# A rational activation's denominator rewritten as a square plus an absolute value, with two changed loading steps ahead of it, in an attention and two-MLP kernel

## The chip, the cores and the metric

The kernel runs on one core of one Trainium2 chip. The metric is the device time of one execution in microseconds (us). The five queues that matter are TensorE (PE), VectorE (DVE), ScalarE (ACT), GpSimd (POOL) and the DMA queue of SyncE (SP).

## What is computed

Local attention with block summaries feeds a first MLP with a rational activation, and that feeds a second MLP with `h*cos(h)`. The part that the change touches is the rational activation and the two block summaries (a maximum over 32 keys, a mean over 32 values).

```python
k_sum = k.reshape(B, H, nb, block, D).max(axis=3)      # B=2 H=8 S=768 D=64 block=32
v_sum = v.reshape(B, H, nb, block, D).mean(axis=3)
...
h = x @ w_in                                           # 1536 x 512 @ 512 x 2048
h2 = h * h
h3 = h2 * h
P = a[0] + a[1] * h + a[2] * h2 + a[3] * h3
Q = 1.0 + np.abs(b[0]) * np.abs(h) + np.abs(b[1]) * h2
g = P / (Q + 1e-06)
return (g @ w_out).astype(np.float32)
```

## The kernel before

**Stages.** Batch 0's keys are loaded and transposed by `k_pair` (L456), batch 1's by `k_tile`; the value means come from `v_mean0` (L512) and `v_mean1` (L540). Twelve attention units of 128 rows each follow (`attn_a`, `attn_b`, `attn_c`): scores, softmax, transposed probabilities, and the product with the values, whose result is split into a high and a low part (xH, xL) as input of the MLP. The MLP works on units: one of 16 column blocks of 128 of the hidden layer, for one of three tiles of 512 tokens, in each of two layers. The first tile's first four blocks are done in halves of 256 tokens, so that layer 0 has 8 half units and 44 full ones, and layer 1 has 48. `mlp_h` (L789) makes 12 matmuls for a unit, `ew1` (L832) or `ew2` the activation, `split_g` the high and low part of the result, and `mlp_o` (L898) 12 more matmuls. The weights arrive as 64-bit floats and are turned to 32-bit ones by three DVE operations (L765, L769, L773) in `conv`, then split into two parts (L360 and L779, mostly on POOL). Attention units are filled in between the MLP units of the first four blocks.

**The activation before.** `ew1` computes `|b1|*|h|` with ACT's Abs out of PSUM (L839), adds `|b0|` and multiplies by `h` on DVE (L847), takes ACT's Abs of that (L855), and then the logarithm (L857) and the exponential of its negative (L860), which is a first value of 1/Q. DVE refines it (L862, L865). The numerator is a chain beside it: L841 (ACT, or DVE as L843), L850, L852, and L868 multiplies both.

**What sets the order.** Nothing is issued in the order in which the code is written. Every step is registered with `P.op`: the engines that may do it with their costs, what it reads, what it writes. A step that lists a tile among its writes comes after every earlier user of that tile. `Plan.order` is a list scheduler: it works out the latest start of each step, then picks steps by when their engine and buffers are free, and among several engines takes the one with the least finish plus a weight per engine that depends on the time (`WEIGHT`). A cost wrapped in `Shared` (certain DVE steps and all POOL steps) also waits until the last such step is over. `setup` is emitted ahead of the plan. TensorE, ACT, DVE, POOL and SP each execute their own list in order.

Of the kernel before, what the change touches and what calls it, by code (L numbers as in the profile page):

```python
# [29 lines left out]
LAT = {}  # L30
# [54 lines left out]
class Op:  # L85
# [2 lines left out]

    def at(self, e):

        return max((t + LAT[x, e] for t, x in self.after), default=0.0)


class Plan:
# [194 lines left out]
def kernel(  # L289
# [21 lines left out]
    WK = 96  # L311
# [52 lines left out]


    nc.scalar.preload_act_table_set("natural_log_exp_and_others")
    co_r = fixed([128, 8], F32, "co")
    co = co_r.t
    ident_r = fixed([128, 128], F32, "ident")
    ident = ident_r.t  # L370
    a0, a1, a2, a3 = (co[:, i:i + 1] for i in range(4))
    b0a, b1a = co[:, 6:7], co[:, 7:8]

    masks = {off: fixed([128, KW], F32, f"mask{off[0]}{off[1]}") for off in ((0, 16), (16, 16), (16, 32))}
    vsel_r = fixed([128, 40], F32, "vsel")
# [7 lines left out]
    def setup():  # L383
        make_identity(nc, ident)

        wu = pools["pa"].tile([128, 512], F32, tag="acc0", name="warm", bufs=1)
        for i in range(8):
            nc.tensor.matmul(out=wu[:, 0:128], lhsT=ident, rhs=ident, start=True, stop=True)
        nc.sync.dma_start(out=co[:, 0:4], in_=moe_a.partition_broadcast(128))
        nc.sync.dma_start(out=co[:, 4:6], in_=moe_b.partition_broadcast(128))  # L390
        nc.scalar.activation(out=co[:, 6:8], in_=co[:, 4:6], func=ACTF.Abs)
        nc.gpsimd.memset(vsel, 0.0)

        nc.gpsimd.memset(vsel[:, 16:24], 1.0 / 32.0)
        nc.gpsimd.affine_select(out=vsel[:, 16:24], in_=vsel[:, 16:24], pattern=[[-16, 8]],
                                compare_op=ALU.is_ge, fill=0.0, base=0, channel_multiplier=1)
        nc.gpsimd.affine_select(out=vsel[:, 16:24], in_=vsel[:, 16:24], pattern=[[16, 8]],
                                compare_op=ALU.is_ge, fill=0.0, base=15, channel_multiplier=-1)
        for offs in masks:
            m = masks[offs].t  # L400
            nc.gpsimd.memset(m, 0.0)
            nc.gpsimd.memset(m[:, WK:KW], LN32_8)
            for half in range(2):
                off = offs[half]
                mh = m[64 * half:64 * half + 64, 0:WK]

# [49 lines left out]
    def k_pair(pr, lead):  # L456

        if pr == 0:
            kT[0] = new("big", [128, 4096], F32, "big", 2)
        kr = kT[0]  # L460
        kk, ks = k_parts(0)
        room = early_room(pr // 2)
        raw = room["k", pr]
        rt = lambda: room.t[:, 768 * (pr % 2):768 * (pr % 2) + 768].rearrange(
            "p (i h x) -> p i h x", i=3, h=2)
        for h in range(2):
            P.op([("S", 0.7)], [], [raw[h]],
                 lambda e, h=h: nc.sync.dma_start(
                     out=rt()[:, :, h], in_=k[0, 2 * pr + h].rearrange("(i s j) d -> s i (j d)", s=128, j=2)),
                 prio=P.now - lead)  # L470
        for i0, n in ((0, 2), (2, 1)):
            tp = psum([128, 256 * n], "ktp", True)

            def tr(e, tp=tp, i0=i0, n=n):
                for i in range(n):
                    transpose_pairs(tp.t[:, 256 * i:256 * i + 256], rt()[:, i0 + i], 0, 128)

            P.op([("T", 0.44 * n)], [raw[0], raw[1]], [tp], tr)
            P.op([("A", act(256 * n, True)), ("V", dve(256 * n))], [],
                 [tp] + [kr["k", i, pr] for i in range(2 * i0, 2 * i0 + 2 * n)],  # L480
                 lambda e, tp=tp, i0=i0, n=n: cp(e, kk()[:, pr, 256 * i0:256 * (i0 + n)], tp.t))
            P.op([("V", dve(256 * n))], [], [tp, kr["s", pr]],
                 lambda e, tp=tp, i0=i0, n=n: nc.vector.tensor_reduce(
                     out=ks()[:, pr, 8 * i0:8 * (i0 + n)],
                     in_=tp.t.rearrange("p (m t) -> p m t", t=32), axis=AX.X, op=ALU.max))
# [26 lines left out]
    def v_mean0(lead):  # L512

        vp = psum([128, NH * D], "vmp", True)
        room = new("big", [128, 4096], F32, "big", 2)
        for i in range(3):
            raw = room[i]
            P.op([("S", 1.75)], [], [raw],
                 lambda e, i=i: nc.sync.dma_start(
                     out=room.t[:, 1024 * i:1024 * i + 1024].rearrange("p (h x) -> p h x", h=NH),  # L520
                     in_=v[0, :, 256 * i:256 * i + 256, :].rearrange("h (s j) d -> s h (j d)", j=2)),
                 prio=P.now - lead)

            def sel(e, i=i):
                x = room.t[:, 1024 * i:1024 * i + 1024].rearrange("p (h j d) -> p h j d", h=NH, j=2)
                for j in range(2):
                    nc.tensor.matmul(out=vp.t[WK:KW].rearrange("p (h d) -> p h d", h=NH),
                                     lhsT=vsel[:, 16 - 8 * i:40 - 8 * i], rhs=x[:, :, j],
                                     start=i == 0 and j == 0, stop=i == 2 and j == 1)

            P.op([("T", 1.78)], [raw], [vp], sel)
        for i in range(2):
            P.op([("A", act(512, True)), ("V", dve(512))], [], [vp, vws[i]["m"]],
                 lambda e, i=i: cp(e, vws[i].t[WK:KW], vp.t[WK:KW]))
        for vw in vws[2:]:
            P.op([("S", 0.2)], [vws[0]["m"]], [vw["m"]],
                 lambda e, vw=vw: nc.sync.dma_start(out=vw.t[WK:KW], in_=vws[0].t[WK:KW]))
        P.now += 5.3

    def v_mean1(lead):  # L540

# [64 lines left out]
    def attn_a(u):  # L606
# [6 lines left out]
               for y in range(NP)}  # L613
        kw = kws[u % NKW]
        if t < NKW:
            P.op([("P", Shared(0.6)), ("A", act(192))], [kr["s", y] for y in range(NP)], [kw["s"]],
                 lambda e: cp(e, kw.t[:, :, :, WK:KW],
                              ks().unsqueeze(2).to_broadcast([128, NP, 2, NB])))

# [26 lines left out]
        for hh in range(2):  # L646
            sc = new("at", [128, NP, KW], F32, "sc", 4)
            sp = sps[hh]
            for pr in range(NP):
# [6 lines left out]
                         out=sc.t[:, pr, :], in_=sc.t[:, pr, :], func=ACTF.Exp, scale=-1.0,  # L656
                         bias=mn.t[:, hh, pr:pr + 1], accum_out=su.t[:, hh, pr:pr + 1]))
            sus = [su[hh, pr] for pr in range(NP)]
            P.op([("A", 0.11)], [], sus,
                 lambda e, hh=hh: nc.scalar.activation(out=su.t[:, hh], in_=su.t[:, hh],  # L660
                                                       func=ACTF.Identity, bias=1e-9))
            P.op([("V", Shared(0.09))], [], sus,
                 lambda e, hh=hh: nc.vector.reciprocal(out=su.t[:, hh], in_=su.t[:, hh]))
            ss = [sc[pr] for pr in range(NP)]
# [167 lines left out]
    def ew1(un):  # L832
# [3 lines left out]
        H, EE, U, Z = (lambda r=r: r.t[:, 0:n] for r in (h, te, tu, tf))  # L836

        P.op([("A", act(n, True, 1))], [], [h, tu],
             lambda e: nc.scalar.activation(out=U(), in_=H(), func=ACTF.Abs, scale=b1a))  # L839
        P.op([("A", act(n, True, 2)), ("V", dve(n, 2))], [], [h, te],  # L840
             lambda e: (nc.scalar.activation(out=EE(), in_=H(), func=ACTF.Identity, scale=a3, bias=a2)  # L841
                        if e == "A" else
                        nc.vector.tensor_scalar(out=EE(), in0=H(), scalar1=a3, scalar2=a2,  # L843
                                                op0=ALU.mult, op1=ALU.add)))

        P.op([("V", dve(n, 1))], [], [h, tu],
             lambda e: nc.vector.scalar_tensor_tensor(out=U(), in0=U(), scalar=b0a, in1=H(),  # L847
                                                      op0=ALU.add, op1=ALU.mult))
        P.op([("V", dve(n))], [], [h, te],
             lambda e: nc.vector.tensor_tensor(out=EE(), in0=EE(), in1=H(), op=ALU.mult))  # L850
        P.op([("V", dve(n, 1))], [], [h, te],
             lambda e: nc.vector.scalar_tensor_tensor(out=EE(), in0=EE(), scalar=a1, in1=H(),  # L852
                                                      op0=ALU.add, op1=ALU.mult))
        P.op([("A", act(n))], [], [tu],
             lambda e: nc.scalar.activation(out=U(), in_=U(), func=ACTF.Abs))  # L855
        P.op([("A", act(n))], [tu], [tf],
             lambda e: nc.scalar.activation(out=Z(), in_=U(), func=ACTF.Ln, bias=QC))  # L857

# [252 lines left out]
```

## Time and profile before

| | us |
|---|---|
| median of 3 runs | 627.66 |
| lowest, highest | 627.12, 629.93 |
| the profiled execution's own time | 628.18 |
| span of its instructions | 626.5 |

| engine | busy us | share of the span |
|---|---|---|
| PE | 602.1 | 96% |
| PE weight load | 493.3 | 79% |
| DVE | 489.0 | 78% |
| ACT | 394.1 | 63% |
| POOL | 352.3 | 56% |

The span runs from the first to the last instruction on the core; some 1.7 us lie around it. Matmuls are pipelined and their ends are modelled, so PE's busy time counts some time in which PE was not at its peak. The mean granted clock of TensorE was 0.986 of full speed.

### The profile page before, as it was taken

To read this page: it belongs to the slowest core of one execution; us is meant where nothing else is said; L and a number is where in the kernel's file an instruction comes from. 1 tells how busy PE (TensorE), PEld (TensorE's weight loads), DVE (VectorE), ACT (ScalarE), POOL (GpSimd) and SP (SyncE) were. 2 spreads that over 40 slices of the span, in tenths; PEclk is the share of its full clock that TensorE was granted. 3 is DMA by queue.
4 is the path that set the end of the run, shared out by engine and by line. 5 is a ranking of instruction groups with operands and counts; after the bars stand their busy time and mean duration, and the time that the engine had idled before them with its cause. 6 is when DMAs were issued, how large, how long until landed. Compare 5 with 4: busy or idle time off the path is not lost.

```text
span 626.5 us, 9893 instructions
## 1 busy us (share of the span) xinstructions
PE 602.1 (96%) x3522; PEld 493.3 (79%) x3522; DVE 489.0 (78%) x942; ACT 394.1 (63%) x851; POOL 352.3 (56%) x368
## 2 busy tenths in 40 slices
PE   8769897999999999999999999999999999999997
PEld 7458876788788888888888878888888888888886
DVE  2599977677999999999999999758756884773541
ACT  4698878967657665766666765454465446543553
POOL 4356684352556676657736668667536764474332
PEclk9889997999999999999999999999999999999999
DMA  8996975210022131213211323313302230000112
GB/s 215 241 225 167 197 192 138 43 22 1 33 69 67 35 104 65 67 35 101 67 35 37 99 67 101 115 54 101 101 0 69 74 129 1 34 1 0 68 49 86
DMA packets 69737, 51.79 MB, mean 83 GB/s; under 512 B 37288, under 2 KB 63912, under 8 KB 69688
## 3 DMA queue, kind: packets, MB, share of 16 engines
q1 hardware_dynamic: 69688, 51.16, 30.2%
q8 instruction: 28, 0.46, 0.3%
q14 instruction: 21, 0.17, 0.1%
HBM read 47.71 MB, written 3.15 MB: 81 GB/s over the span
## 4 chain that ended last, share of the span: by engine, by line
PE 74%; DVE 14%; ACT 5%; SPq 3%; DMA 2%; issue 1%; POOL 0%; DVEq 0%
PE acc L929 36%; PE h L805 35%; DMA raw<-in_moe_w_in_dram 2%; DVE f L765 1%; DVE f L773 1%; DVE tu L847 1%; DVE f L769 1%; PE sp L637 1%; DVE sc L651 1%; DVE te L850 1%; PE avp L727 1%; DVE tu L862 1%; DVE te L868 1%; DVE h L865 1%; DVE te L852 1%
## 5 line engine op out<-in xcount | busy, mean ns | idle before, releaser
L805 PE MATMUL h<-xH,w 128*128 128x512 f32 (+1 forms) x544 | 173.2, 380 | 1.6 <-DVE te L868 0.9
L360 POOL TENSOR_SCALAR gh<-te 128x512 fp32r<-128x512 f32 (+1 forms) x89 | 61.1, 686 | 153.2 <-DVE te L892 77.0
L824 POOL TENSOR_TENSOR gl<-te,gh 128x512 fp32r<-128x512 f32 (+1 forms) x100 | 136.8, 1369 | 7.0 <-ACT gh L358 0.2
L929 PE MATMUL acc<-gh,w 128*128 128x512 f32 (+1 forms) x416 | 122.0, 377 | 0.0
L929 PE MATMUL acc<-w,gh 128*128 128x512 f32 x384 | 118.5, 390 | 0.9 <-DVE xL L951 0.9
L805 PEld LDWEIGHTS h<-xH,w 128*128 128x128 f32 x544 | 100.5, 188 | 21.8 <-DVE te L868 1.1
L805 PE MATMUL h<-xL,w 128*128 128x512 f32 (+1 forms) x272 | 102.7, 378 | 0.2 <-DVE xL L738 0.2
L805 PE MATMUL h<-big,w 128*128 128x512 f32 x384 | 92.2, 390 | 1.4 <-DVE te L868 1.4
L884 DVE SCALAR_TENSOR_TENSOR h<-tu,h 128x512 f32<-128x512 int32 x96 | 66.4, 691 | 34.3 <-ACT te L358 33.2
L929 PEld LDWEIGHTS acc<-gh,w 128*128 128x128 f32 x416 | 75.4, 188 | 14.9 <-issue 1.2
L805 PEld LDWEIGHTS h<-big,w 128*128 128x128 f32 x384 | 72.0, 188 | 16.9 <-DVE te L868 1.8
L779 POOL TENSOR_TENSOR w<-f,w 128x512 fp32r<-128x512 f32 x62 | 83.4, 1347 | 3.2
L929 PEld LDWEIGHTS acc<-w,gh 128*128 128x128 f32 x384 | 72.1, 188 | 16.2 <-DVE xL L951 1.3
L929 PE MATMUL acc<-gl,w 128*128 128x512 f32 (+1 forms) x208 | 77.7, 374 | 0.0
L929 PE MATMUL acc<-w,gl 128*128 128x512 f32 x192 | 74.8, 389 | 0.0
L360 POOL TENSOR_SCALAR w<-f 128x512 fp32r<-128x512 f32 x49 | 31.7, 650 | 69.6 <-DVE f L773 45.8
L887 ACT ACTIVATE h<-h 128x512 f32<-128x512 f32 x48 | 27.9, 582 | 65.9 <-DVE h L884 65.9
L805 PEld LDWEIGHTS h<-xL,w 128*128 128x128 f32 x272 | 51.2, 188 | 9.4 <-DVE xL L738 0.4
L892 DVE TENSOR_TENSOR te<-te,h 128x512 f32<-128x512 f32 x48 | 32.9, 685 | 32.7 <-ACT h L889 32.5
L879 ACT ACTIVATE tu<-h 128x512 int32<-128x512 f32 x48 | 28.7, 598 | 45.2 <-PE h L805 45.1
L769 DVE SCALAR_TENSOR_TENSOR f<-raw,f 128x512 int32<-128x512 int32 x64 | 52.1, 815 | 0.5
L773 DVE SCALAR_TENSOR_TENSOR f<-raw,f 128x512 int32<-128x512 int32 x64 | 51.9, 812 | 0.6
(93 smaller groups left out, 975.9 us busy)
## 6 DMA issues: line engine op xcount, KB each, us to landing
raw<-in_moe_w_in_dram SPq DMA_DIRECT2D x32, 512.0 KB, 3.8
raw<-in_moe_w_out_dram SPq DMA_DIRECT2D x32, 512.0 KB, 6.9
vw<-in_v_dram SPq DMA_DIRECT2D x24, 192.0 KB, 4.0
qk<-in_q_dram SPq DMA_DIRECT2D x10, 256.0 KB, 5.0
out_dram<-part SPq DMA_DIRECT2D x8, 256.0 KB, 3.2
part<-in_k_dram SPq DMA_DIRECT2D x8, 192.0 KB, 4.6
big<-in_v_dram SPq DMA_DIRECT2D x3, 512.0 KB, 6.3
qk<-in_k_dram SPq DMA_DIRECT2D x6, 256.0 KB
```

Source lines behind the costliest of these rows:

```text
L360: nc.gpsimd.tensor_scalar(out=o, in0=i, scalar1=1.0, scalar2=1.0, op0=ALU.mult, op1=ALU.mult)
L637: nc.tensor.matmul(out=sps[hh].t[c0:c0 + 64, pr, :], lhsT=qt.t[p0:p0 + 64, pr, c0:c0 + 64], rhs=kw.t[p0:p0 + 64, pr, half, :], start=True, ...
L769: lambda e, lohi=lohi, ft=ft: nc.vector.scalar_tensor_tensor(out=ft.t.bitcast(I32), in0=lohi()[1], scalar=-0x40000000, in1=ft.t.bitcast(I3 ...
L773: lambda e, lohi=lohi, ft=ft: nc.vector.scalar_tensor_tensor(out=ft.t.bitcast(I32), in0=lohi()[0], scalar=29, in1=ft.t.bitcast(I32), op0=A ...
L779: lambda e, ft=ft, w=w: E[e].tensor_tensor(out=w.t[:, 1, :], in0=ft.t, in1=w.t[:, 0, :].bitcast(F32), op=ALU.subtract),
L805: nc.tensor.matmul(out=h.t[:, 0:n], lhsT=lt, rhs=rt[:, kk, cs], start=(k0 == 0 and i == 0), stop=(k0 == 2 and i == 5))
L824: lambda e: E[e].tensor_tensor(out=un.gl.t[:, 0:n], in0=g.t[:, 0:n], in1=un.gh.t[:, 0:n].bitcast(F32), op=ALU.subtract))
L879: lambda e: nc.scalar.activation(out=K().bitcast(I32), in_=H(), func=ACTF.Identity, scale=1.0 / (2.0 * math.pi)))
L884: lambda e, c=c: nc.vector.scalar_tensor_tensor(out=H(), in0=K().bitcast(I32), scalar=-c, in1=H(), op0=ALU.mult, op1=ALU.add))
L887: lambda e: nc.scalar.activation(out=H(), in_=H(), func=ACTF.Abs))
L892: lambda e: nc.vector.tensor_tensor(out=S_(), in0=S_(), in1=H(), op=ALU.mult))
L929: nc.tensor.matmul(out=dst, lhsT=lt, rhs=rt, start=(un.start and not have and i == 0), stop=(un.stop and i == 2), skip_group_check=have)
```

## The change

It has six parts. (1) `ew1`: ACT squares `h` with the scale `sqrt(|b1|)` into `tu`, ACT takes the absolute value of `b0*h` into `tf`, and a plain addition of the two tiles in SBUF, on POOL or DVE, replaces L847; the Abs of L855 goes, so `tf` is taken up by each unit from its second step on. (2) `setup` computes the square root of `|b1|` in seven small steps on ACT and DVE, and the two small loads of the coefficients go from SP's queue to ACT's. (3) `k_pair` loads each pair of heads in two halves of the sequence instead of by head, with runs of three rows (768 bytes) instead of two (512 bytes), still eight loads of 192 KB; a transposition waits for one load instead of two. (4) `v_mean0` adds the two rows of a run on POOL or DVE before the product, as `v_mean1` does, so that three products stand where six stood. (5) The addition of 1e-9 to the softmax sums may also go to DVE. (6) A margin table in the scheduler, all of whose values are 0.0.

```diff
-        nc.sync.dma_start(out=co[:, 0:4], in_=moe_a.partition_broadcast(128))
-        nc.sync.dma_start(out=co[:, 4:6], in_=moe_b.partition_broadcast(128))
-        nc.scalar.activation(out=co[:, 6:8], in_=co[:, 4:6], func=ACTF.Abs)
+        nc.scalar.dma_start(out=co[:, 0:4], in_=moe_a.partition_broadcast(128))
+        nc.scalar.dma_start(out=co[:, 4:6], in_=moe_b.partition_broadcast(128))
+
+        nc.scalar.activation(out=co[:, 7:8], in_=co[:, 5:6], func=ACTF.Abs)
+        nc.vector.tensor_scalar(out=co[:, 8:9], in0=co[:, 7:8], scalar1=1e-30, scalar2=None, op0=ALU.max)
+        nc.scalar.activation(out=co[:, 8:9], in_=co[:, 8:9], func=ACTF.Ln)
+        nc.scalar.activation(out=co[:, 8:9], in_=co[:, 8:9], func=ACTF.Exp, scale=0.5)
+        nc.vector.reciprocal(out=co[:, 9:10], in_=co[:, 8:9])
+        nc.vector.scalar_tensor_tensor(out=co[:, 9:10], in0=co[:, 9:10], scalar=co[:, 7:8],
+                                       in1=co[:, 8:9], op0=ALU.mult, op1=ALU.add)
+        nc.vector.tensor_scalar(out=co[:, 8:9], in0=co[:, 9:10], scalar1=0.5, scalar2=None, op0=ALU.mult)
...
-        for h in range(2):
-            P.op([("S", 0.7)], [], [raw[h]],
-                 lambda e, h=h: nc.sync.dma_start(
-                     out=rt()[:, :, h], in_=k[0, 2 * pr + h].rearrange("(i s j) d -> s i (j d)", s=128, j=2)),
-                 prio=P.now - lead)
-        for i0, n in ((0, 2), (2, 1)):
...
-            P.op([("T", 0.44 * n)], [raw[0], raw[1]], [tp], tr)
...
+        for i in range(2):
+            raw = room["k", pr, i]
...
+            P.op([("S", 0.62)], [], [raw],
+                 lambda e, i=i, rt=rt: nc.sync.dma_start(
+                     out=rt(), in_=k[0, 2 * pr:2 * pr + 2, 384 * i:384 * i + 384].rearrange(
+                         "h (s j) d -> s h (j d)", j=3)), prio=P.now - lead)
+            tp = psum([128, 384], "ktp", True)
...
+            P.op([("T", 0.78)], [raw], [tp], tr)
...
-                for j in range(2):
-                    nc.tensor.matmul(out=vp.t[WK:KW].rearrange("p (h d) -> p h d", h=NH),
-                                     lhsT=vsel[:, 16 - 8 * i:40 - 8 * i], rhs=x[:, :, j],
-                                     start=i == 0 and j == 0, stop=i == 2 and j == 1)
-
-            P.op([("T", 1.78)], [raw], [vp], sel)
+            P.op([("P", pool(512)), ("V", dve2(512))], [], [raw],
+                 lambda e, x=x: E[e].tensor_tensor(out=x()[:, :, 0], in0=x()[:, :, 0], in1=x()[:, :, 1],
+                                                   op=ALU.add))
+            P.op([("T", 0.89)], [raw], [vp],
...
         P.op([("A", act(n, True, 1))], [], [h, tu],
-             lambda e: nc.scalar.activation(out=U(), in_=H(), func=ACTF.Abs, scale=b1a))
+             lambda e: nc.scalar.activation(out=U(), in_=H(), func=ACTF.Square, scale=b1s))
+        P.op([("A", act(n, True, 1))], [], [h, tf],
+             lambda e: nc.scalar.activation(out=Z(), in_=H(), func=ACTF.Abs, scale=b0))
...
-        P.op([("V", dve(n, 1))], [], [h, tu],
-             lambda e: nc.vector.scalar_tensor_tensor(out=U(), in0=U(), scalar=b0a, in1=H(),
-                                                      op0=ALU.add, op1=ALU.mult))
+        P.op([("P", pool(n)), ("V", dve2(n))], [tf], [tu],
+             lambda e: E[e].tensor_tensor(out=U(), in0=U(), in1=Z(), op=ALU.add))
...
-        P.op([("A", act(n))], [], [tu],
-             lambda e: nc.scalar.activation(out=U(), in_=U(), func=ACTF.Abs))
```

## Rows read from the trace of the kernel before

**Rows 1.** The page, busy time, share of the span and instructions.

```profile
PE 602.1 (96%) x3522; PEld 493.3 (79%) x3522; DVE 489.0 (78%) x942; ACT 394.1 (63%) x851; POOL 352.3 (56%) x368
```

**Rows 2.** Stages: length, busy PE, PEld, DVE, ACT, POOL, clock, DMA share, GB/s.

```profile
26.00:82.00 56.00, 47.52 (x567) 40.75 (x568) 53.54 (x178) 47.04 (x167) 32.76 (x39) 0.91 0.88 197
82.00:104.00 22.00, 18.70 (x205) 13.91 (x203) 17.13 (x59) 16.66 (x49) 14.82 (x14) 0.91 0.85 217
104.00:162.00 58.00, 55.32 (x466) 44.20 (x465) 42.40 (x112) 46.55 (x127) 23.97 (x26) 0.98 0.10 22
162.00:322.00 160.00, 160.00 (x708) 132.56 (x707) 154.48 (x242) 102.65 (x169) 100.63 (x96) 1.00 0.21 66
322.00:376.00 54.00, 53.09 (x233) 43.13 (x232) 53.12 (x85) 38.55 (x67) 31.22 (x30) 1.00 0.19 59
```

**Rows 3.** Chain that ended last, in time: start, us, what.

```profile
17.50 8.41 DMA raw<-in_moe_w_in_dram
...
59.51 0.39 DVE tu L847
...
91.19 0.66 DVE tu L847
```

**Rows 4.** Waits of PE, from 140 to 165 us and from 350 to 380 us.

```profile
PE h L805 <- DVE te L868: 1.4, 1, 1.4
...
PE acc L929 <- DVE xL L951: 0.9, 1, 0.9
```

**Rows 5.** Timeline of the first 16 us: start, us, engine, line.

```profile
0.80 1.28 ACT L366 ACT_TABLE_LOAD   x1 [0.80 <-PEq L1095]
...
1.24 0.42 SPq L390 DMA_DIRECT2D co<-in_moe_b_dram  x1
...
1.70 4.87 SPq L468 DMA_DIRECT2D part<-in_k_dram  x8
...
5.45 0.20 ACT L391 ACTIVATE co<-co 128x2 f32<-128x2 f32 x1 [3.37 <-DMA co<-in_moe_b_dram]
...
7.91 0.86 ACT L358 COPY big<-ktp 128x512 f32<-128x512 f32 x2 [2.25 <-PE ktp L446]
...
14.53 1.88 PE L527 MATMUL vmp<-big,vsel 128*24 128x512 f32 x4
```

**Rows 6.** Groups by form on DVE, from 26 to 82 us: busy, mean ns.

```profile
L773 DVE SCALAR_TENSOR_TENSOR f<-raw,f 128x512 int32<-128x512 int32 x9 | 6.8, 768 | 0.0
L765 DVE TENSOR_SCALAR f<-raw 128x512 int32<-128x512 int32 x10 | 5.6, 563 | 2.3 <-DMA raw<-in_moe_w_in_dram 1.7 <-DMA raw<-in_moe_w_out_dram 0.6
...
L847 DVE SCALAR_TENSOR_TENSOR tu<-tu,co,h 128x256 f32<-128x256 f32 x8 | 3.8, 476 | 0.6 <-ACT te L841 0.6
```

**Rows 7.** Two DVE lines alone, whole run: ns min/median/max.

```profile
L765 DVE TENSOR_SCALAR f<-raw x64: 412/430/1527, 25.9 to 557.5; 128x512 int32<-128x512 int32 x64
...
L773 DVE SCALAR_TENSOR_TENSOR f<-raw,f x64: 664/686/1797, 27.1 to 561.3; 128x512 int32<-128x512 int32 x64
```

**Rows 8.** Groups by form on POOL, whole run: busy, mean ns.

```profile
L824 POOL TENSOR_TENSOR gl<-te,gh 128x256 fp32r<-128x256 f32 x8 | 6.9, 859 | 0.3
...
L550 POOL TENSOR_TENSOR raw<-raw 128x512 f32<-128x512 f32 x3 | 3.9, 1299 | 0.0
```

**Rows 9.** Groups by form on ACT and DVE, whole run: busy, mean ns.

```profile
L847 DVE SCALAR_TENSOR_TENSOR tu<-tu,co,h 128x512 f32<-128x512 f32 x44 | 32.6, 740 | 5.5 <-ACT te L841 5.3
...
L839 ACT ACTIVATE tu<-h,co 128x512 f32<-128x512 f32 x44 | 30.1, 684 | 18.7 <-PE h L805 18.5
...
L855 ACT ACTIVATE tu<-tu 128x512 f32<-128x512 f32 x44 | 28.0, 637 | 30.9 <-DVE tu L847 30.8
```

**Rows 10.** Timeline around 78 us, POOL and DVE.

```profile
77.72 1.30 POOL L550 TENSOR_TENSOR raw<-raw 128x512 f32<-128x512 f32 x1
...
78.12 1.45 DVE L773 SCALAR_TENSOR_TENSOR f<-raw,f 128x512 int32<-128x512 int32 x1
```

**Rows 11.** Busy time and clock from 100 to 105 us, columns as in rows 2.

```profile
100.00:105.00 5.00, 4.23 (x41) 3.22 (x38) 4.28 (x20) 3.38 (x14) 2.49 (x4) 0.50 0.57 123
```

More of the change, by code (lines that the diff above doesn't have):

```diff
@@ L39 @@
 DMAQ = 2.0
+MT, MV, MS = 0.0, 0.0, 0.0
+MARGIN = {(d, e): (MT if e == "T" else MV) + (MS if d else 0.0) for d in (False, True) for e in "AVPTS"}
 SLACK = 0.3
@@ L89, in at @@
     def at(self, e):
-        return max((t + LAT[x, e] for t, x in self.after), default=0.0)
+        return max((t + LAT[x, e] + MARGIN[x == "S", e] for t, x in self.after), default=0.0)
 class Plan:
@@ L366 @@
     nc.scalar.preload_act_table_set("natural_log_exp_and_others")
-    co_r = fixed([128, 8], F32, "co")
+    co_r = fixed([128, 12], F32, "co")
     co = co_r.t
@@ L371 @@
     a0, a1, a2, a3 = (co[:, i:i + 1] for i in range(4))
-    b0a, b1a = co[:, 6:7], co[:, 7:8]
+    b0, b1s = co[:, 4:5], co[:, 8:9]
     masks = {off: fixed([128, KW], F32, f"mask{off[0]}{off[1]}") for off in ((0, 16), (16, 16), (16, 32))}
@@ L462, in k_pair @@
         room = early_room(pr // 2)
-        raw = room["k", pr]
-        rt = lambda: room.t[:, 768 * (pr % 2):768 * (pr % 2) + 768].rearrange(
-            "p (i h x) -> p i h x", i=3, h=2)
-        for h in range(2):
-            P.op([("S", 0.7)], [], [raw[h]],
-                 lambda e, h=h: nc.sync.dma_start(
-                     out=rt()[:, :, h], in_=k[0, 2 * pr + h].rearrange("(i s j) d -> s i (j d)", s=128, j=2)),
-                 prio=P.now - lead)
-        for i0, n in ((0, 2), (2, 1)):
[L472 to L476, printed above, removed]
-            P.op([("T", 0.44 * n)], [raw[0], raw[1]], [tp], tr)
[L479 to L484, printed above, removed]
@@ new lines, in k_pair, with tr @@
+        for i in range(2):
+            raw = room["k", pr, i]
+            o0 = 768 * (pr % 2) + 384 * i
+            rt = lambda o0=o0: room.t[:, o0:o0 + 384].rearrange("p (h x) -> p h x", h=2)
+            P.op([("S", 0.62)], [], [raw],
[3 more added lines that the diff above has]
+            tp = psum([128, 384], "ktp", True)
+            def tr(e, tp=tp, rt=rt):
+                for j in range(3):
+                    for h in range(2):
+                        o = tp.t[D * h:D * h + D].rearrange("p (s j) -> p s j", j=3)
+                        nc.tensor.matmul(out=o[:, :, j], lhsT=rt()[:, h, D * j:D * j + D],
+                                         rhs=ident, start=True, stop=True)
+            P.op([("T", 0.78)], [raw], [tp], tr)
+            P.op([("A", act(384, True)), ("V", dve(384))], [],
+                 [tp] + [kr["k", x, pr] for x in range(3 * i, 3 * i + 3)],
+                 lambda e, tp=tp, i=i: cp(e, kk()[:, pr, 384 * i:384 * i + 384], tp.t))
+            P.op([("V", dve(384))], [], [tp, kr["s", pr, i]],
+                 lambda e, tp=tp, i=i: nc.vector.tensor_reduce(
+                     out=ks()[:, pr, 12 * i:12 * i + 12],
@@ L485, in k_pair @@
                      in_=tp.t.rearrange("p (m t) -> p m t", t=32), axis=AX.X, op=ALU.max))
-            P.now += 0.44 * n
+            P.now += 0.78
     def k_tile(i, lead):
@@ L522, in v_mean0 @@
                  prio=P.now - lead)
-            def sel(e, i=i):
-                x = room.t[:, 1024 * i:1024 * i + 1024].rearrange("p (h j d) -> p h j d", h=NH, j=2)
-                for j in range(2):
-                    nc.tensor.matmul(out=vp.t[WK:KW].rearrange("p (h d) -> p h d", h=NH),
-                                     lhsT=vsel[:, 16 - 8 * i:40 - 8 * i], rhs=x[:, :, j],
-                                     start=i == 0 and j == 0, stop=i == 2 and j == 1)
-            P.op([("T", 1.78)], [raw], [vp], sel)
+            x = lambda i=i: room.t[:, 1024 * i:1024 * i + 1024].rearrange("p (h j d) -> p h j d", h=NH, j=2)
+            P.op([("P", pool(512)), ("V", dve2(512))], [], [raw],
+                 lambda e, x=x: E[e].tensor_tensor(out=x()[:, :, 0], in0=x()[:, :, 0], in1=x()[:, :, 1],
+                                                   op=ALU.add))
+            P.op([("T", 0.89)], [raw], [vp],
+                 lambda e, i=i, x=x: nc.tensor.matmul(
+                     out=vp.t[WK:KW].rearrange("p (h d) -> p h d", h=NH),
+                     lhsT=vsel[:, 16 - 8 * i:40 - 8 * i], rhs=x()[:, :, 0],
+                     start=i == 0, stop=i == 2))
         for i in range(2):
@@ L537, in v_mean0 @@
                  lambda e, vw=vw: nc.sync.dma_start(out=vw.t[WK:KW], in_=vws[0].t[WK:KW]))
-        P.now += 5.3
+        P.now += 2.7
     def v_mean1(lead):
@@ L615, in attn_a @@
         if t < NKW:
-            P.op([("P", Shared(0.6)), ("A", act(192))], [kr["s", y] for y in range(NP)], [kw["s"]],
+            P.op([("P", Shared(0.6)), ("A", act(192))], [kr[x] for x in kr.subs if x[0] == "s"], [kw["s"]],
                  lambda e: cp(e, kw.t[:, :, :, WK:KW],
@@ L658, in attn_a @@
             sus = [su[hh, pr] for pr in range(NP)]
-            P.op([("A", 0.11)], [], sus,
-                 lambda e, hh=hh: nc.scalar.activation(out=su.t[:, hh], in_=su.t[:, hh],
-                                                       func=ACTF.Identity, bias=1e-9))
+            P.op([("A", 0.11), ("V", 0.08)], [], sus,
+                 lambda e, hh=hh: (nc.scalar.activation(out=su.t[:, hh], in_=su.t[:, hh],
+                                                        func=ACTF.Identity, bias=1e-9) if e == "A" else
+                                   nc.vector.tensor_scalar(out=su.t[:, hh], in0=su.t[:, hh], scalar1=1e-9,
+                                                           scalar2=None, op0=ALU.add)))
             P.op([("V", Shared(0.09))], [], sus,
```

## The prediction

> **What bounds the kernel now.** I read the page's busy times first. PE is busy 96% of the span [rows 1], and the first thing to settle is where the rest lies, since only there can a lighter activation buy time. The busy times by stage answer it [rows 2]. From 162 to 322 us PE is busy all 160.00 us: DVE is nearly full beside it (154.48), but nothing can be gained while PE is the bound. From 26 to 82 us it is the other way round: DVE is busy 53.54 of 56 us and PE 47.52, at a mean granted clock of 0.91. There the attention units, the weight conversion and the first half units all ask for DVE. From 82 to 104 the bound changes hands, with DVE at 17.13 of 22. From 104 to 162 PE has 55.32 of 58 and DVE 42.40, and from 322 to 376 DVE is full again (53.12 of 54) while PE misses 0.9.
>
> The chain of work that ended last says the same in order of time: up to 17.5 us it is SP's queue and then the landing of the first weights, 8.41 us long [rows 3]; from there to some 95 us DVE pieces prevail, L847 among them; from 104 on PE's. The waits of PE give the two late losses: 1.4 us for DVE's L868 near 158 us and 0.9 us for DVE's L951 near 370 us [rows 4].
>
> **The change part by part.** The sum is made against the profiled execution's own 628.18 us (span 626.5); the median shown is 627.66, 0.52 lower.
>
> *Start.* The two coefficient loads leave SP's queue. The first key load is issued at 1.70 us behind them [rows 5], and would be at 0.80, where the first of them stands now: -0.9 us for all that follows on SP, up to the weights that the chain waits for. Larger runs (two thirds as many) could shorten the issue of the eight key loads, 4.87 us, by up to a third, which makes -2.5 the one bound. The other end: ACT's load starts only after its table load (0.80 + 1.28 = 2.08) and the second one about 0.4 later, at 2.5. It landed 4.2 us after its issue (1.24 to 5.45), so 6.7; Abs, maximum, logarithm and exponential at 0.2 each (the Abs took 0.20 [rows 5]) with their handovers end near 7.7. ACT's first copy of keys starts at 7.91 now, so the copies hardly lose, but they can't use the earlier keys either. If those loads take as long as the weights took (8.41 [rows 3]), ACT is free 4 us later, near 12: bound +4. I take -0.9, the nearest row being the small load itself.
>
> *The DVE step L847.* From 26 to 82 us there are 8 of it, mean 476 ns [rows 6]; the next step starts under its tail, so that one holds the chain for 0.39 [rows 3]: -3.1 us. In its place stand 8 additions that the scheduler will mostly give to POOL. The trace has no such addition of 256 columns, the nearest is POOL's subtraction of the low part, 859 ns [rows 8]; for 512 columns it is the addition of `v_mean1`, 1299 ns, on the same engine with the same operands. POOL has 32.76 us of work in these 56, so 8 x 0.86 = 6.9 fit. But they slow DVE. L773 took 1.45 us at 78.12 while POOL's L550 ran from 77.72 [rows 10], against a median of 0.686 [rows 7]. In this stage L773 and L765 exceed their medians by 9 x 0.082 + 10 x 0.133 = 2.1 us [rows 6, 7], which is 6% of POOL's 32.76; 6.9 more POOL time then costs 0.4 to 0.5. Net -2.6; bounds -3.8 (the full durations of eight) and +3.8 (every addition holding DVE up for its whole length, -3.1 + 6.9).
>
> The Trainium skill's page "SBUF — State Buffer", section "SBUF: two separate sides", says that a DVE operation with two SBUF inputs and a GpSimd operation exclude each other, the later one blocking until the earlier ends. The stretched L773 agrees. By this rule taken at its worst the term would be the +3.8 bound; the trace's mean share of 6% says how seldom they meet.
>
> *82 to 104.* One L847 is on the chain, 0.66 us [rows 3]: -0.7, bounds 0 and -0.7. *Near 158.* DVE is late by 1.4 us after the attention has ended [rows 4], and L847 comes there once a unit with 740 ns [rows 9]: -1.4, bounds -2.2 (three units' worth) and 0. *Near 370.* DVE is late by 0.9 with L847 in every unit ahead: -0.9, bounds -0.9 and 0.
>
> *162 to 322.* Nothing, as long as POOL holds: at 12 + 12 matmuls or about 5.4 us a unit, 29 units add 29 x 1.3 = 38 us to POOL's 100.63, 139 of 160; DVE, relieved of 29 x 0.74 = 21 us, can take some. PE's full queue hides it all. If POOL fell behind, the gl part that PE's second product waits for would be late.
>
> *ACT.* Five steps a unit before and after. An Abs from SBUF (637 ns) goes and one from PSUM with a scale per partition comes (684 as L839) [rows 9]: 0.05 more, hidden by ACT's gaps (47.04 busy of 56). Square does not occur in the trace. Nearest is L839, the same engine, shape, source and scale: 0.68. It costs at least what the Abs it replaces costs, as far as rows tell, so 0; were it outside the loaded table, 1.28 [rows 5] twice a unit over 52 units, 133 us, is the upper end, which I hold at 1 in 100 since Abs, Identity, Ln and Exp go side by side without a second load in layer 0. [...]
>
> *Value means.* Two products of 512 columns took 1.88 us [rows 5], so three loads save 2.8 us of PE, and three additions of 1.3 on POOL come ahead of them. Both lie beside SP's queue and the landing weights: 0, bounds -2.8 and +1.3. *The rest*: the 1e-9 step (0.2 us, either engine), the zero margins, and `tf`, which two units may now hold from the second step on (so that the third unit would have to be late for it to matter): 0, each within 1 us either way. The scheduler renews the whole order, which is good for 1 to 2 us in either direction.
>
> Sum: -0.9 - 2.6 - 0.7 - 1.4 - 0.9 = -6.5, so 621.7 against 628.18, and 621.2 against the median. The new late one I expect in 26 to 104 us is ACT, with 47.04 + 16.66 of 78 us.
>
> **The rivals.** *More than the sum.* The clock is a second prize. From 100 to 105 us it was 0.50, the 1.2 GHz level, with PE busy for 4.23 of 5 us only [rows 11]; over the first three stages of rows 2 the shares missing from 2.4 GHz are 56 x 0.09 + 22 x 0.09 + 58 x 0.02 = 8.2 us. If DVE's relief closes half of those gaps, 4 us more: 617. Against it: ACT's softmax, not DVE, made some of these waits.
>
> *Absorbed.* ACT and the weights' DMA take DVE's place between 26 and 104, where they are nearly as full (DMA share 0.88 and 0.85 [rows 2]), and the start gives 0.4: -0.4 - 1.4 - 0.9 = -2.7, so 625.0.
>
> *It does not do what it says.* The scheduler puts the additions on DVE, where two SBUF inputs cost about what L847 cost; only the start remains: 626.8.
>
> *Slower: POOL against DVE.* The place is the port where L769 and L773 meet POOL's additions, from 26 to 162 us. The price is up to an addition's length: 8 x 0.86 + 10 x 1.30 = 20 us in all there, behind which the softmax scaling and the split of g also queue. At a share of one third, 6.5 us, it eats the whole gain; at 55% it is 11, 4.7 over: 632.4. For it: rows 10. Against it: today's share is 6%, and POOL has gaps.
>
> **How the numbers follow.** Chances: the sum 0.42, more 0.17, absorbed 0.20, not done 0.06, POOL 0.15 (a slow Square among it). About 0.5%, 3.1 us, can be told from no change, so faster means below 624.5 and slower above 630.8. The sum's own range is 618 to 624.5, all but 0.02 of it faster; more is faster; absorbed gives 0.03 faster and 0.01 slower; not done is the same but for 0.01; POOL gives 0.14 slower and 0.01 same. Faster 0.60, same 0.24, slower 0.16. The predicted time is the sum's. For the range I reach down past 617 by the start's bound, and up through absorbed and not done to where POOL begins to win: 613.5 to 630.5.
>
> **What would show it.** Right: DVE clearly below 53 of 56 us in the stage from 26 on, additions on POOL of 0.8 and 1.3 us, the first key load issued near 0.8, no PE wait for DVE near 158 and 370, PE still full in the middle. Wrong: additions on DVE; L769 and L773 with means near 1 us; ACT's first key copy well after 8 us; table loads inside layer 0; or ACT at 9 tenths and more from 26 to 104 with PE's gaps as before.

## The result and the profile after

The kernel after takes 618.53 us (median of 4, 618.03 to 618.96); the kernel before, with one more run beside it, 627.89. The ratio is 0.9837 with a 95% interval of 0.9819 to 0.9855: 9.4 us less than the 627.89, 9.1 less than the 627.66 shown above. The forecast was 621.2 with a range of 613.5 to 630.5.

The page's first part, and busy time by stage, columns as in [rows 2]:

```profile
PE 595.5 (97%) x3516; PEld 489.9 (79%) x3516; DVE 477.8 (77%) x919; ACT 396.4 (64%) x842; POOL 413.7 (67%) x409
```

```profile
26.00:82.00 56.00, 47.80 (x557) 40.77 (x556) 51.64 (x172) 47.53 (x151) 45.76 (x50) 0.97 0.85 225
82.00:104.00 22.00, 20.70 (x272) 16.98 (x272) 16.91 (x77) 20.91 (x72) 13.26 (x14) 1.00 0.47 130
104.00:162.00 58.00, 55.06 (x381) 43.79 (x380) 43.97 (x100) 42.14 (x97) 39.72 (x37) 0.97 0.12 33
162.00:322.00 160.00, 160.00 (x706) 132.06 (x706) 149.68 (x216) 109.21 (x183) 131.30 (x115) 1.00 0.20 63
322.00:376.00 54.00, 53.56 (x236) 43.96 (x235) 50.56 (x77) 34.39 (x60) 44.46 (x40) 1.00 0.25 78
```

Against [rows 1, 2]: POOL has taken on 61.4 us, and PE is still full from 162 to 322. DVE, which lost 52 steps of L847 (36.4 us), is down by only 11.2, and in the stage from 26 to 82 us it is still at 51.64 of 56. The granted clock is 0.97, 1.00 and 0.97 in the first three stages where it was 0.91, 0.91 and 0.98. From 82 to 104 ACT and PE are now about equally full (20.91 and 20.70 of 22).

The timeline of the start (start, us, engine, line):

```profile
0.80 1.28 ACT L368 ACT_TABLE_LOAD   x1 [0.80 <-PEq L1109]
...
0.81 5.76 SPq L478 DMA_DIRECT2D part<-in_k_dram  x8
0.83 0.43 ACTq L391 DMA_DIRECT2D co<-in_moe_a_dram  x1
...
1.29 0.49 ACTq L392 DMA_DIRECT2D co<-in_moe_b_dram  x1
...
6.38 0.20 ACT L394 ACTIVATE co<-co 128x1 f32<-128x1 f32 x1 [4.30 <-DMA co<-in_moe_b_dram]
...
7.14 1.79 ACT L360 COPY big<-ktp 128x384 f32<-128x384 f32 x4
```

The first key load is issued 0.9 us earlier than in [rows 5], ACT's first key copy starts 0.8 us earlier. PE's waits for DVE near 158 us and near 370 us, the answer to [rows 4]:

```profile
PE h L820 <- DVE te L882: 0.9, 1, 0.9
```

```profile
PE acc L943 <- DVE xL L965: 0.4, 1, 0.4
```

Three milestones make the traces comparable: PE's first product of the MLP, ACT's second table load (the first Sin, where layer 1 begins), and the end of the span. The first two, before and then after:

```profile
35.42 0.38 PE L805 MATMUL h<-xH,w 128*128 128x256 f32 x1
...
361.00 1.28 ACT L889 ACT_TABLE_LOAD   x1
```

```profile
31.09 0.38 PE L820 MATMUL h<-xH,w 128*128 128x256 f32 x1
...
352.18 1.28 ACT L903 ACT_TABLE_LOAD   x1
```

The three stood at 35.4, 361.0 and 626.5 us before and stand at 31.1, 352.2 and 616.8 after. So 4.3 us were won before the MLP began, 4.5 more within layer 0, and 0.9 in layer 1.

### The profile page after: what moved, and what is told of

Its sections match the earlier page's. It is cut to its first block, busy times and chain, and to the rows that moved or that the text cites. A ratio compares the mean times of both kernels' runs of the same rounds, so it can differ in the third digit from the quotient of the medians.

```text
span 616.8 us, 9933 instructions
## 1 busy us (share of the span) xinstructions
PE 595.5 (97%) x3516; PEld 489.9 (79%) x3516; DVE 477.8 (77%) x919; ACT 396.4 (64%) x842; POOL 413.7 (67%) x409
## 4 chain that ended last, share of the span: by engine, by line
PE 61%; DVE 20%; ACT 9%; POOL 4%; issue 3%; DMA 3%; SPq 0%; DVEq 0%; ACTq 0%; POOLq 0%
PE acc L943 29%; PE h L820 28%; ACT sc L668 2%; DVE te L868 2%; DVE tu L876 2%; DVE h L879 2%; DVE te L866 2%; DVE te L882 2%; DVE f L784 2%; DVE f L788 2%; DVE f L780 2%; ACT h L874 1%; PE avp L742 1%; POOL tu L864 1%; DMA big<-in_v_dram 1%
## 5 line engine op out<-in xcount | busy, mean ns | idle before, releaser
L839 POOL TENSOR_TENSOR gl<-te,gh 128x512 fp32r<-128x512 f32 (+1 forms) x100 | 135.0, 1350 | 7.4 <-ACT gh L360 0.9
L362 POOL TENSOR_SCALAR gh<-te 128x512 fp32r<-128x512 f32 (+1 forms) x84 | 59.3, 706 | 100.9 <-DVE te L906 80.9
L943 PE MATMUL acc<-gh,w 128*128 128x512 f32 (+1 forms) x416 | 123.5, 380 | 1.3 <-POOL gh L362 1.3
L864 POOL TENSOR_TENSOR tu<-tu,tf 128x512 f32<-128x512 f32 (+1 forms) x52 | 67.1, 1291 | 19.6 <-ACT tf L856 19.5
L906 DVE TENSOR_TENSOR te<-te,h 128x512 f32<-128x512 f32 x48 | 32.9, 685 | 35.1 <-ACT h L903 34.9
L784 DVE SCALAR_TENSOR_TENSOR f<-raw,f 128x512 int32<-128x512 int32 x64 | 56.1, 877 | 0.5
L788 DVE SCALAR_TENSOR_TENSOR f<-raw,f 128x512 int32<-128x512 int32 x64 | 56.0, 875 | 0.6
```

The source lines that it names most:

```text
L362: nc.gpsimd.tensor_scalar(out=o, in0=i, scalar1=1.0, scalar2=1.0, op0=ALU.mult, op1=ALU.mult)
L784: lambda e, lohi=lohi, ft=ft: nc.vector.scalar_tensor_tensor(out=ft.t.bitcast(I32), in0=lohi()[1], scalar=-0x40000000, in1=ft.t.bitcast(I3 ...
L788: lambda e, lohi=lohi, ft=ft: nc.vector.scalar_tensor_tensor(out=ft.t.bitcast(I32), in0=lohi()[0], scalar=29, in1=ft.t.bitcast(I32), op0=A ...
L839: lambda e: E[e].tensor_tensor(out=un.gl.t[:, 0:n], in0=g.t[:, 0:n], in1=un.gh.t[:, 0:n].bitcast(F32), op=ALU.subtract))
L864: lambda e: E[e].tensor_tensor(out=U(), in0=U(), in1=Z(), op=ALU.add))
L906: lambda e: nc.vector.tensor_tensor(out=S_(), in0=S_(), in1=H(), op=ALU.mult))
```

## The experiments

The theory is the sum: the activation's relief of DVE brings most (5.6 of 6.5 us), the start the rest. The first rival gives the start nearly half. The second says that the scheduler's new order, which any edit brings about, is worth as much as the edit. In the sessions of the experiments the kernel before took 628.6 to 628.7 us; the ratios are against runs on the same chip.

**The activation alone, and the loading alone.** The first takes the hunks of `ew1` and `setup` into the kernel before. Against these hunks it differs in that the two coefficient loads stay on SP:

```diff
-        nc.scalar.dma_start(out=co[:, 0:4], in_=moe_a.partition_broadcast(128))
-        nc.scalar.dma_start(out=co[:, 4:6], in_=moe_b.partition_broadcast(128))
+        nc.sync.dma_start(out=co[:, 0:4], in_=moe_a.partition_broadcast(128))
+        nc.sync.dma_start(out=co[:, 4:6], in_=moe_b.partition_broadcast(128))
```

> The kernel before with the new activation and its coefficient set-up alone; the coefficient loads stay on SP's queue, the key loads and the value means are as before. The prediction's sum (5.6 of its 6.5 us from the activation): 622.3, with PE's first MLP product near 35.4 us as before. Rival, that the earlier start (PE's first MLP product at 31.1 us after, 35.4 before) carries nearly half of the 9.4 us: 622.5 to 624, which is close, so the companion run decides. Rival, that the gain is an accident of the scheduler's new order: anywhere from 618 to 630, with stalls in other places than DVE's.

The second takes the hunks of `k_pair`, `v_mean0` and the summaries' reads, and moves the coefficient loads:

```diff
-        nc.sync.dma_start(out=co[:, 0:4], in_=moe_a.partition_broadcast(128))
-        nc.sync.dma_start(out=co[:, 4:6], in_=moe_b.partition_broadcast(128))
+        nc.scalar.dma_start(out=co[:, 0:4], in_=moe_a.partition_broadcast(128))
+        nc.scalar.dma_start(out=co[:, 4:6], in_=moe_b.partition_broadcast(128))
         nc.scalar.activation(out=co[:, 6:8], in_=co[:, 4:6], func=ACTF.Abs)
```

> The kernel before with the coefficient loads on ACT's queue, the key loads by halves of the sequence, and the halved value means; the old activation. The prediction's sum gives it 0.9 us: 627.0. Rival, that the start carries 4.3 us (35.4 to 31.1): 623.6, with PE's first MLP product near 31 us. Rival, that DVE, full from 26 us on, takes the early start back: first product near 31 us but 626 to 628 at the end.

Measured: 626.55 (0.9966, 0.9949 to 0.9982) and 626.44 (0.9966, 0.9949 to 0.9983). Each comes out about 2.1 us below the kernel before, and their sum is less than half of the change's gain. Neither run has part (5), the step for 1e-9 that may go to DVE, and no run takes that part by itself. The first product came at 34.0 and 33.2 us: in neither as early as after, and earlier even where no load had been touched. Of the 2.2 us by which it is early with the loading alone, that run's trace has 0.9 left where layer 1 begins and at the end (360.1 and 625.6 us against 361.0 and 626.5); the traced execution took 627.32, longer than the median, so whether an engine takes the rest back stays open. What the activation brings falls far short of 5.6.

**The addition pinned to DVE.**

```diff
-        P.op([("P", pool(n)), ("V", dve2(n))], [tf], [tu],
+        P.op([("V", dve2(n))], [tf], [tu],
```

> The kernel after, but the addition of the square and the absolute value may only go to DVE, 52 times. If DVE's relief is what the activation brings, the relief is gone and it loses 4 to 6 us against the kernel after: 622.5 to 624.5. Rival, that the shorter chain of dependent steps brings it (one Abs less behind the DVE step): within 1 us of 618.5. Rival, POOL against DVE at their shared port: faster than after, below 617.5.

Measured: 627.52 (0.9977, 0.9959 to 0.9996), some 9 us over the kernel after and well above what the theory allows. That is more than DVE's relief was ever thought to bring. The scheduler makes a new order for this kernel too, and the run can't tell that from the addition's place.

**The same work in another order.** SLACK is the margin, in us, by which the scheduler puts the latest start of every step outside TensorE earlier.

```diff
-SLACK = 0.3
+SLACK = 0.35
```

> The kernel before with one constant of the scheduler moved a little (SLACK from 0.30 to 0.35); the work is the same, only the order of steps and the choice of engines differ. If the prediction's allowance for a renewed order is right, it stays within 2 us of 627.9. Rival, that the order alone is worth as much as the change: 4 us or more away on either side.

Measured: 620.73 (0.9868, 0.9849 to 0.9886). What is computed is the same, step by step; only the order and, for some steps, the engine differ, and most of the change's gain is there. Its stages, columns as in [rows 2]:

```profile
26.00:82.00 56.00, 46.70 (x570) 40.27 (x570) 51.62 (x178) 47.88 (x169) 36.67 (x40) 0.94 0.92 201
82.00:104.00 22.00, 19.30 (x251) 14.06 (x252) 16.66 (x57) 17.77 (x62) 12.63 (x13) 1.00 0.81 209
104.00:162.00 58.00, 56.93 (x445) 45.93 (x440) 49.11 (x122) 47.44 (x121) 28.65 (x31) 1.00 0.13 31
...
322.00:376.00 54.00, 54.00 (x238) 44.24 (x237) 53.26 (x86) 37.98 (x65) 35.81 (x33) 1.00 0.25 78
```

The two late losses that the prediction hung on L847 are absent with every L847 in place: PE has 56.93 of 58 from 104 on with no wait for L868, and misses nothing from 322 to 376 although DVE is as full there as before. In the first of these stages DVE is at 51.62 of 56, which is what it has after the change; PE's busy time is no higher there than before (46.70 against 47.52), at a clock of 0.94 in place of 0.91. The milestones are 33.8, 354.9 and 620.0.

**Order and work apart.** The next two keep a kernel's order step by step and exchange the activation's instructions in it. Before's order with the new activation and its set-up of the coefficients (one more buffer for `tf`, so that no wait for it comes in):

```diff
...
-             lambda e: nc.scalar.activation(out=U(), in_=H(), func=ACTF.Abs, scale=b1a))
+             lambda e: (nc.scalar.activation(out=U(), in_=H(), func=ACTF.Square, scale=b1s),
+                        nc.scalar.activation(out=Z(), in_=H(), func=ACTF.Abs, scale=b0)))
...
-             lambda e: nc.vector.scalar_tensor_tensor(out=U(), in0=U(), scalar=b0a, in1=H(),
-                                                      op0=ALU.add, op1=ALU.mult))
+             lambda e: nc.gpsimd.tensor_tensor(out=U(), in0=U(), in1=Z(), op=ALU.add))
...
-             lambda e: nc.scalar.activation(out=U(), in_=U(), func=ACTF.Abs))
+             lambda e: None)
```

> The order of the kernel before kept step by step; only the activation's instructions are the new ones in it: Square and Abs in the place of the first Abs, the addition on GpSimd in the place of the DVE step, nothing in the place of the second Abs. If the work itself is what counts (the prediction's step), DVE's relief shows without any help from a new order: 621 to 624 (4 to 6 us under 627.9). Rival, order: no gain beyond the 1 to 2 us of e1, or a loss, since the order was made for other durations: 626 to 630.

After's order with the old activation:

```diff
...
-             lambda e: nc.scalar.activation(out=U(), in_=H(), func=ACTF.Square, scale=b1s))
+             lambda e: nc.scalar.activation(out=U(), in_=H(), func=ACTF.Abs, scale=b1a))
...
-             lambda e: nc.scalar.activation(out=Z(), in_=H(), func=ACTF.Abs, scale=b0))
+             lambda e: None)
...
-             lambda e: E[e].tensor_tensor(out=U(), in0=U(), in1=Z(), op=ALU.add))
+             lambda e: nc.vector.scalar_tensor_tensor(out=U(), in0=U(), scalar=b0a, in1=H(),
+                                                      op0=ALU.add, op1=ALU.mult))
...
-             lambda e: nc.scalar.activation(out=Z(), in_=U(), func=ACTF.Ln, bias=QC))
+             lambda e: (nc.scalar.activation(out=U(), in_=U(), func=ACTF.Abs),
+                        nc.scalar.activation(out=Z(), in_=U(), func=ACTF.Ln, bias=QC)))
```

> The order of the kernel after kept step by step, loading included, with the old activation's instructions in it: the old DVE step in the place of the addition, the second Abs right before the logarithm. If the work counts, this loses most of the activation's part against the kernel after: 622.5 to 625. Rival, order: it keeps most of the 9.4 us, 618 to 621.

Measured: 636.89 (1.0139, 1.0118 to 1.0160) and 639.39 (1.0184, 1.0159 to 1.0210). Neither side's expectation held.

| | old activation | new activation |
|---|---|---|
| before's order | 628.7 | 636.9 |
| after's order and loading | 639.4 | 618.5 |

Each order fits its own instructions and loses with the other's. In before's order ACT's logarithm stands behind the new addition; the largest waits of ACT in that run (waiter, awaited, us in total, times, longest):

```profile
ACT h L895 <- DVE h L892: 61.9, 43, 2.7
ACT tu L887 <- PE h L813: 49.3, 40, 1.7
ACT tf L865 <- POOL tu L856: 41.9, 27, 4.3
```

The first two belong to layer 1, where nothing was exchanged; the third is the new step. In the kernel before ACT stood behind L847 at the same place for 31.1 us, so 10.8 are new; that these are what made the kernel slower is not shown. In after's order with the old steps PE, which misses nothing from 162 to 322 us in either kernel, starves (columns as in [rows 2]):

```profile
165.00:220.00 55.00, 53.01 (x225) 43.06 (x225) 51.83 (x80) 35.75 (x60) 30.50 (x30) 0.97 0.15 49
220.00:280.00 60.00, 59.46 (x262) 48.91 (x261) 56.26 (x85) 38.56 (x63) 30.86 (x30) 1.00 0.21 65
280.00:340.00 60.00, 56.54 (x239) 45.20 (x238) 56.56 (x88) 39.67 (x66) 30.84 (x30) 0.97 0.18 59
```

It is not that DVE is too full. From 220 to 280 us it is busy for 56.26 us, as long as in the kernel after and less than in the kernel before (58.05), and in neither of these does PE miss anything there. From 165 to 340 us PE's waits in this run are for copies of its partial sums (`acc`, `part`) by DVE and ACT, 5.8 us in all, and none is for a step of the activation. So an order fits only its own steps, and to exchange them costs 8.2 us in the one and 20.9 in the other. What these two can't say is how good an order the old work could have had, and the run with 0.35 has said it: 620.7.

**More draws of orders.** The other five only move SLACK, in the kernel before (to 0.25 and 0.40) and in the kernel after (to 0.25, 0.35 and 0.40).

```diff
-SLACK = 0.3
+SLACK = 0.25
```

> The kernel before with SLACK moved the other way, from 0.30 to 0.25. If before's order was an unlucky one and 620.7 is nearer to usual, this comes at 619 to 625. If the order with 0.35 was the lucky one, 626 to 631.

> The kernel after with SLACK at 0.35. If the change's work is worth some 6 us at any order, this comes well under the 620.7 of the old work with 0.35: 612 to 616. If it is worth 2 us, the value of e1 and e2 each, 617 to 620, near the kernel after. If after's own order was a lucky one, 621 to 626.

> The kernel after with SLACK at 0.25. With 618.5 at 0.30 and 626.9 at 0.35 on record: if the work is worth a few us over all orders, the mean of the kernels after at several values lies some 4 us under that of the kernels before (632.4, 628.7, 620.7, mean 627.3), so this one at 617 to 626. If the order is all, as likely above 627 as below.

> The kernel before with SLACK at 0.40, one more draw of an order for the old work: 620 to 633, by the spread so far. If 620.7 at 0.35 was a trend of the constant and not an accident, 616 to 621.

> The kernel after with SLACK at 0.40, one more draw for the new work: 616 to 628. With e10, e11 and the earlier draws it gives four values on each side; the work counts if the mean of these is 3 us or more under that of the old work's.

Medians in us, ratio to the kernel before in brackets:

| SLACK | work of before | work of after |
|---|---|---|
| 0.25 | 632.43 (1.0064, 1.0045 to 1.0083) | 628.29 (0.9979, 0.9959 to 0.9999) |
| 0.30 | 1 by definition | 618.53 (0.9837, 0.9819 to 0.9855) |
| 0.35 | 620.73 (0.9868, 0.9849 to 0.9886) | 626.88 (0.9977, 0.9965 to 0.9990) |
| 0.40 | 623.86 (0.9915, 0.9900 to 0.9931) | 629.75 (1.0023, 1.0004 to 1.0041) |
| mean ratio | 0.9962 | 0.9954 |

The old work spreads over 11.7 us and the new over 11.2. The means differ by 0.0008, or 0.5 us. The standard deviations of the four are 5.2 and 5.0 us, so the difference of the means is known to about 3.6 us (the root of 5.2² / 4 + 5.0² / 4) as a standard error. By the bound set for the last run, 3 us between the means, the work of the change does not stand out from the orders; an advantage of some us, or a disadvantage, isn't excluded either. The best of each side, 620.73 and 618.53, are 2.2 us apart. As far as these runs show, the 9.4 us are the distance between two draws, a poor one before and the best of eight after.

**The clock.** The kernel before in its own order, with matmuls of the identity in front of three waits; their results are overwritten.

```diff
+            for _ in range({2: 9, 8: 20}.get(u, 0)):
+                nc.tensor.matmul(out=sps[0].t[:, 0, :], lhsT=ident, rhs=ident[:, 0:KW], start=True, stop=True)
...
+            for _ in range({0: 13}.get(u, 0)):
+                nc.tensor.matmul(out=op.t[:, 0, :], lhsT=ident, rhs=ident, start=True, stop=True)
```

> The kernel before, its order unchanged, with matmuls of the identity into score and output tiles that are overwritten right after, where PE waits for ACT or DVE: 13 ahead of attention unit 0's output, 9 ahead of unit 2's scores and 20 ahead of unit 8's (waits of 1.5, 1.0 and 2.4 us). If the granted clock that falls behind such waits costs time by itself, the stages 25 to 35 and 100 to 110 us come back to 1.00 and the time falls by 1.5 to 3 us: 625.5 to 627. Rival, the low clock only sits where PE has nothing urgent: the clock rises, the time stays within 0.7 us. Rival, the added matmuls stand in PE's way: 1 to 3 us slower.

Measured: 629.67 (1.0016, 1.0003 to 1.0030), 1.0 us slower. The stage of [rows 11] with the fill, and its timeline around unit 8's scores:

```profile
100.00:105.00 5.00, 4.58 (x63) 4.06 (x62) 2.52 (x14) 2.41 (x8) 2.76 (x3) 1.00 0.94 204
```

```profile
98.32 4.70 PE L634 MATMUL sp<-ident 128*128 128x120 f32 x40
102.94 1.05 PE L639 MATMUL sp<-kw,qT 64*64 64x120 f32 x32
...
111.04 0.50 PE L809 MATMUL h<-xH,w 128*128 128x512 f32 x1
```

The same stretch of the kernel before:

```profile
99.26 1.35 PE L637 MATMUL sp<-kw,qT 64*64 64x120 f32 x30 [2.41 <-ACT qT L358]
...
109.31 0.51 PE L805 MATMUL h<-xH,w 128*128 128x512 f32 x1
```

The clock came back from 0.50 (the 1.2 GHz level) to 1.00. The fill was twice too long, 4.70 us in a wait of 2.4, and unit 8's scores began 3.7 us late. Of these 3.7 us 1.8 were there ahead of it: PE's last step before the fill stands at 97.59 us, against 95.75 in the kernel before. The next MLP product came 1.7 us late. From the scores to this product the same attention steps took 10.05 us before and 8.10 with the fill, with one wait of 0.77 us in either, so the low clock had cost some 2 us there, and at this place the fill neither won nor lost. The loss lies ahead of it: behind the two other fills the first MLP product stands at 37.4 us, 2.0 later than before.

## Why the prediction was right, and by what

The number was right and inside the likeliest case's own range (618 to 624.5). The sum behind it was not what made it: with SLACK at 0.25, 0.35 or 0.40 the same change takes 626.88 to 629.75 us, and only at 0.30 does it come near the forecast. That the two agree is luck. One step failed outright: "The scheduler renews the whole order, which is good for 1 to 2 us in either direction." The orders drawn with one constant span 11.7 us for the old work and 11.2 for the new. Against this, terms of -0.7 to -2.6 us can't be told apart by total times, and the wait for L868 near 158 us and the one for L951 near 370, which the sum priced one by one, belonged to the order: in the run with 0.35 the stage from 322 to 376 is full with L847 still in it. In the kernel after both waits are still there, at 0.9 and 0.4 us, so that 0.5 us was won at each where 1.4 and 0.9 had been put. The remark that the order would be renewed stood in the text; it should have been the widest bound and a rival of its own.

*Start, -0.9.* SP's first key load moved from 1.70 to 0.81 us as put, but the path behind it was wrong. The key loads' issue did not shrink with the fewer runs, it grew (4.87 to 5.76 us), so that all eight were out at 6.57 us in both kernels and the 0.9 us were gone there. Wrong was also that ACT's load has to wait for the table load: ACT issued it at 0.83 and 1.29, inside the 1.28 us of L368. What was won came later: the first load of weights was issued at 17.50 us before, at 17.43 with the loading alone and at 15.61 after, and its conversion began at 25.9, 23.8 and 21.0. The loading alone had the first product 2.2 us earlier (35.4 to 33.2); the other 2.1 of the 4.3 us in the kernel after came only with the rest of the edit, in its new order. Orders move this milestone too: over the four values of SLACK its mean is 35.1 us with the old work and 32.9 with the new, 2.2 apart with a standard error of 1.1, and where layer 1 begins the means are 359.7 and 359.5, with a standard error of 3.9, so that no gain can be seen any more.

*L847, -2.6, and the three later terms.* Where the step went is as predicted: all 52 additions are on POOL, with the expected durations (859 and 1299 ns were taken). By form on POOL, then the three DVE lines of `conv` and the step for 1e-9:

```profile
L864 POOL TENSOR_TENSOR tu<-tu,tf 128x512 f32<-128x512 f32 x44 | 60.2, 1368 | 16.9 <-ACT tf L856 16.8
...
L864 POOL TENSOR_TENSOR tu<-tu,tf 128x256 f32<-128x256 f32 x8 | 6.9, 868 | 2.7 <-ACT tf L856 2.7
```

```profile
L784 DVE SCALAR_TENSOR_TENSOR f<-raw,f 128x512 int32<-128x512 int32 x64 | 56.1, 877 | 0.5
L788 DVE SCALAR_TENSOR_TENSOR f<-raw,f 128x512 int32<-128x512 int32 x64 | 56.0, 875 | 0.6
L780 DVE TENSOR_SCALAR f<-raw 128x512 int32<-128x512 int32 x64 | 43.4, 684 | 5.3 <-POOL w L794 5.3
...
L675 DVE TENSOR_SCALAR su<-su 128x4 f32<-128x4 f32 x21 | 7.5, 355 | 3.2 <-ACT sc L668 3.1
```

The same three lines of `conv` in the kernel before:

```profile
L769 DVE SCALAR_TENSOR_TENSOR f<-raw,f 128x512 int32<-128x512 int32 x64 | 52.1, 815 | 0.5
L773 DVE SCALAR_TENSOR_TENSOR f<-raw,f 128x512 int32<-128x512 int32 x64 | 51.9, 812 | 0.6
L765 DVE TENSOR_SCALAR f<-raw 128x512 int32<-128x512 int32 x64 | 43.1, 678 | 11.2 <-POOL w L779 5.8 <-DMA raw<-in_moe_w_in_dram 4.7 <-DMA raw<-in_moe_w_out_dram 0.6
```

Here is where the relief went. Of the 36.4 us that left DVE, the first two of these lines took 8.1 back, and 7.5 came with the step for 1e-9, which the scheduler moved to DVE 21 of 24 times and which the prediction costed at nothing. More copies and the value sums took some more. By single durations DVE has 17.6 us less; its busy time, which counts steps that overlap once, is down by 11.2. The port was sized at 6% of POOL's added time over the stage from 26 on; over the run the 8.1 us on these two lines alone are 12% of the 67.1 us of additions.

That POOL's additions stretch the conversions is shown where the order stands still: by the exchange of the activation's instructions alone the three lines together go from 147.1 to 157.9 us in before's order, and from 155.5 down to 146.7 in after's. In every kernel with the additions on POOL (51 or 52 of the 52) they take 155.5 to 164.2 us, in every other 144.7 to 147.1, the one with the addition pinned to DVE among these. Over the four values of SLACK the means are 145.8 and 160.0: 14 of the 36.4 us come back there, about a fifth of the additions' 67.1 us. From 26 to 82 us, where the sum counted on DVE's relief most, DVE is busy for 51.7 us on average with the old work and 51.8 with the new, so the 1.9 us less of the pair shown (53.54 to 51.64) can't be put down to the work. This is the rival "POOL against DVE" in kind, short of the third at which it would have eaten the gain. (In that rival's price 11 - 6.5 is 4.5 and not 4.7.)

*162 to 322, ACT, Square.* Right: PE stayed full there with POOL at 131.30 of 160 (139 was the estimate). With SLACK moved the new work is less safe there: PE is busy for 158.13, 157.31 and 159.62 of the 160 us, the old work for 159.53 or more. Right too: the two table loads of the run are L368 and L903, none inside layer 0; the Square of 512 columns took 682 ns where 0.68 us was taken.

*The rivals.* The clock gain of the rival "more" did happen beside the sum: the shares missing from 2.4 GHz in the first three stages fell from 8.2 to 56 x 0.03 + 58 x 0.03 = 3.4 us. It isn't the change's own either: the old work with 0.35 has 0.94, 1.00 and 1.00, which is 3.4 us as well. How much of the 9.4 us is the clock and how much is waits stays open.

The part that is settled: from ACT's second table load to the end it takes 264.6 us after and 265.5 before, and between 262.7 and 267.3 in the experiments, while that table load itself stands anywhere from 352.2 to 372.0 us. So the time of any of these kernels is mostly decided by how well start and layer 0 are packed. Which property of an order packs them well was not found.

## What to carry to other kernels

Where a scheduler writes the order, first measure what the order alone is worth: move a constant that leaves what is computed as it is, a few times on either side, and take that spread as the noise of every edit. Then compare means over several orders, or the best of each, and don't credit a part with a gain that one pair of kernels shows. A step taken off a full engine comes back as stretched neighbours and as other steps that the scheduler moves in, so its price has to be read from the engine's net busy time.

## What had not been expected of the hardware

ACT issued two DMAs while its table load was running (L391 at 0.83 us, the load from 0.80 to 2.08), so the table load did not hold the queue's issues up. And a DVE step over four columns was stretched by POOL: L675, with a median of 173 ns, ran up to 1087. Of its first ten, the four that took more than 0.2 us (0.35 to 0.95) end 0.02 to 0.03 us after a POOL step that was running beside them; one of 0.14 us, at 39.78, was not held although a POOL step is recorded from 39.73. The first of the four ends at 19.73 us, POOL's step at 19.71:

```profile
18.73 0.98 POOL L681 TENSOR_TENSOR sc<-sc,su 128x480 f32<-128x480 f32 x1
...
19.24 0.49 DVE L675 TENSOR_SCALAR su<-su 128x4 f32<-128x4 f32 x1
```

The Trainium skill's page "SBUF — State Buffer", section "SBUF: two separate sides", has the exclusive lock of the shared port cover DVE operations in a 2-port mode as well as those with two SBUF inputs; these rows agree that one SBUF input is enough.
